# The last two loads of w2 in a decode kernel, each issued as two loads over parts of the partitions

## The chip, the core and the metric

The kernel runs on one core of a Trainium2 chip. The time is device time in microseconds (us) of that core for one execution. The core has a matrix engine (TensorE: PE for its products, PEld for the loading of its stationary operand), VectorE (DVE), ScalarE (ACT), GpSimd (POOL) and SyncE (SP), which here issues the transfers. Transfers between HBM and the on-chip memory are carried by 16 DMA engines. The on-chip memory has 128 partitions.

## The reference

One decode step for two batch rows: grouped attention over the last W = 4096 positions of a cache, a Mish feed-forward layer, and a gate that mixes the two.

```python
W = min(4096, max(256, Sk // 4))
q = (x @ wq) as (B, 32 heads, 1, 128)
k = jnp.repeat(k_cache[:, :, Sk - W:, :], 4, axis=1)
v = jnp.repeat(v_cache[:, :, Sk - W:, :], 4, axis=1)
p = softmax(einsum("bhqd,bhkd->bhqk", q, k) * Dh ** -0.5)
a = einsum("bhqk,bhkd->bhqd", p, v) as (B, 1, 4096) @ wo
h = x @ w1 + b1
b = (h * tanh(softplus(h))) @ w2
g = sigmoid((x * gate_w).sum(-1))
out = g * a + (1 - g) * b
```

All is float32. w2 is 1792 by 512: 14 blocks (f = 0 to 13) of 128 rows, and a block is 256 KB.

## The kernel before

Some 91 MB have to be read, and the kernel is a stream of loads that SP issues in the order of the program: wq in two halves, a small tile, w1, then for each of eight key/value heads a K and a V tile of 4 MB, then w2 and wo. A big load writes a tile of 128 partitions from one of five stream buffers; SP issues it when the buffer's last readers are done.

The end of the stream is cut ever finer, so that little work is left behind the last byte: `w2_0` (blocks 0 to 9 of w2, 2.5 MB), wo in four pieces (`wo0` 4 MB, `wo4` 2 MB, `wo6` and `wo7` 1 MB each), and then the tail of w2 in three pieces that have their own tiles and wait for no buffer: `w2_10` (blocks 10 and 11, 512 KB), `w2_12` and `w2_13` (one block, 256 KB each). CUTS holds these cuts of w2. In such a load a partition gets one contiguous run, 2 KB in the last two.

TensorE follows in the same order. `project` sums the products with w2_0 and wo into `acc`, four column groups side by side. When wo7's products are done, ACT and then DVE copy half of `acc` each into `asum`. `finish` sums into a second accumulator, `fin`: first the eight products with w2_10, then four that fold asum in, then four with w2_12, then four with w2_13. Four small copies (DVE and ACT in turn) bring fin into `res`, and SP issues the store of res to `out`.

Each load signals its arrival on one of eight semaphores (here DMAHW0 to DMAHW7), which the loads take in turn; SP issues a load on a semaphore only when the load that had it before has arrived. The row names below leave the numbers out: `w` is a piece of w1 or w2, `wo` a piece of wo.

Of the kernel before, what the change touches and what calls it, by code (L numbers as in the profile page):

```python
# [13 lines left out]
P = 128  # L14
# [20 lines left out]
SMALL = DC * B + DC + FC  # L35
SCALE = DH ** -0.5
CUTS = (0, 10, 12, 13, 14)


@with_exitstack  # L40
def decode_kernel(ctx: ExitStack, tc: tile.TileContext, small, wq, kt, v, wo, w1, w2, out):
    nc = tc.nc
# [8 lines left out]
    def load(src, cols, name):  # L51
        t = stream.tile([P, CHUNK], F32, tag="s", name=name)
        nc.sync.dma_start(t[:, :cols], src)  # L53
        return t
# [90 lines left out]
    def values(kv, pT, t):  # L145
        o = ps_1.tile([P, BN, DH], F32, tag="o", name=f"o{kv}")
        for c in range(NT):
            for j in range(NJ):
                nc.tensor.matmul(o[Q * j : Q * j + Q], pT[:, c, Q * j : Q * j + Q],  # L149
                                 t[:, (c * NJ + j) * 512 : (c * NJ + j + 1) * 512],  # L150
                                 start=(c == 0), stop=(c == NT - 1))
        d = od[:, kv, :]
        nc.vector.tensor_scalar_mul(d, o[:, 0, :], pick[:, 0:1])  # L153
        for m in range(1, BN):
            nc.vector.scalar_tensor_tensor(d, o[:, m, :], pick[:, m : m + 1], d,  # L155
                                           op0=ALU.mult, op1=ALU.add)
# [98 lines left out]
    def load_w2(i):  # L255
        f0, f1 = CUTS[i], CUTS[i + 1]
        src = w2[f0 * P * D : f1 * P * D].rearrange("(p x) -> p x", p=P)
        if i == 0:
            return load(src, (f1 - f0) * D, f"w2_{f0}")
        t = const.tile([P, (f1 - f0) * D], F32, name=f"w2_{f0}")  # L260
        nc.sync.dma_start(t, src)
        return t

    def load_wo(k0, k1):
        return load(wo[k0 * REP * D * P : k1 * REP * D * P].rearrange("(p x) -> p x", p=P),
                    (k1 - k0) * REP * D, f"wo{k0}")

    w2_0 = load_w2(0)
    wos = [(k0, k1, load_wo(k0, k1)) for k0, k1 in ((0, 4), (4, 6), (6, 7), (7, 8))]
    tail = [load_w2(i) for i in range(1, len(CUTS) - 1)]  # L270

    acc = ps_1.tile([P, D], F32, tag="acc", name="acc")
# [3 lines left out]
    def project(j, lhsT, rhs, n):  # L276
        nc.tensor.matmul(acc[Q * j : Q * j + Q, :], lhsT, rhs,  # L277
                         start=(n_col[j] == 0), stop=(n_col[j] == n - 1))
        n_col[j] += 1

    n_of = [HKV + len(range(j, CUTS[1], NJ)) for j in range(NJ)]
    n_fin = FC - CUTS[1] + 1
    done = [0]
# [11 lines left out]
    values(HKV - 1, pT, last_v)  # L295
    for f in range(CUTS[1]):
        project(f % NJ, actT[:, f, :], w2_0[:, f * D : (f + 1) * D], n_of[f % NJ])
# [10 lines left out]
    def output(i):  # L308
        for f in range(CUTS[i], CUTS[i + 1]):
            x = (f - CUTS[i]) * D  # L310
            finish(actT[:, f, :], tail[i - 1][:, x : x + D])
# [53 lines left out]
```

## Time and profile before

| | us |
|---|---|
| median of 3 runs | 221.48 (221.29 to 222.4) |
| the profiled execution, its own time | 221.49 |
| its span, first to last instruction | 219.70 |
| TensorE busy in the span | 123.8 (56%) |
| VectorE busy | 36.5 (17%) |
| ScalarE busy | 9.1 (4%) |
| DMA queue of the loads, share of 16 engines | 96.8% |

The own time is 1.79 us more than the span, for what lies before the first and behind the last instruction. The busy times overlap; the last line says how much of the span the 16 DMA engines had packets of the loads under way. Two things are to be looked up in such a profile for a change at the end of a stream: when the last bytes arrive, and what the engines do between that and the last instruction.

### The profile page before, as it was taken

Reading aid. Unit: us, or ns where it says so; the run is one execution under the profiler, and the core shown is the slowest. Engines: PE = TensorE matmul, PEld = TensorE weight load, DVE = VectorE, ACT = ScalarE, POOL = GpSimd, SP = SyncE. Lnnn points to the kernel's source line nnn. Section 1 sums busy time; section 2 is a strip of 40 time slices with the busy share of each in tenths; the row PEclk is TensorE's granted clock in tenths of the full one; section 3 lists DMA queues with packets and bytes.
Section 4 is the critical chain, followed back from the end, with each engine's and each line's share of the span. In section 5 each row is a group of like instructions: output and inputs, shape, how many; then the busy total and the mean of one; then the engine's idle time right before and its main releaser. Section 6 shows DMA issues by size and latency. Waiting matters only on the chain.

```text
span 219.7 us, 1885 instructions
## 1 busy us (share of the span) xinstructions
PE 123.8 (56%) x798; PEld 37.0 (17%) x798; DVE 36.5 (17%) x132; ACT 9.1 (4%) x23; POOL 3.0 (1%) x9
## 2 busy tenths in 40 slices
PE   0058638265473628576392752668474655695763
PEld 0012212012120201211020120112011111521112
DVE  1011212411202200120202112011211205302001
ACT  2000000010001000100100010010001001000001
POOL 5000000000000000000000000000000000000000
PEclk9999988887969976676969799585888879679999
DMA  7999999999999999999999999999999999999990
GB/s 280 406 462 397 454 431 427 441 419 465 400 465 394 462 400 459 412 447 430 430 444 418 453 412 453 406 465 403 453 406 453 424 436 407 440 462 403 409 381 22
DMA packets 4043, 91.35 MB, mean 416 GB/s; under 512 B 578, under 2 KB 578, under 8 KB 964
## 3 DMA queue, kind: packets, MB, share of 16 engines
q1 hardware_dynamic: 4036, 91.25, 96.8%
q8 instruction: 6, 0.10, 0.2%
q14 instruction: 1, 0.01, 0.0%
HBM read 91.24 MB, written 0.00 MB: 415 GB/s over the span
## 4 chain that ended last, share of the span: by engine, by line
DMA 80%; PE 15%; DVE 2%; ACT 1%; SPq 1%; issue 1%; DVEq 0%
DMA k<-in_kt 40%; DMA w<-in_w 21%; DMA v<-in_v 19%; PE sc L130 5%; PE o L149 4%; PE hp L208 2%; PE ol L195 1%; PE fin L287 1%; SPq L53 1%; ACT p L137 0%; DVE mx L133 0%; DVE pT L142 0%; PE pp L141 0%; DVE res L321 0%; DVE r L188 0%
## 5 line engine op out<-in xcount | busy, mean ns | idle before, releaser
L130 PE MATMUL sc<-k,qz 128*32 128x512 f32 x256 | 43.1, 836 | 36.1 <-DMA k<-in_kt 36.1
L149 PE MATMUL o<-v,pT 128*32 128x512 f32 x256 | 40.5, 790 | 12.1 <-DMA v<-in_v 11.3
L130 PEld LDWEIGHTS sc<-k,qz 128*32 128x32 f32 x256 | 9.9, 147 | 68.8 <-DMA k<-in_kt 42.8
L149 PEld LDWEIGHTS o<-v,pT 128*32 128x32 f32 x256 | 10.5, 140 | 36.6 <-issue 34.0
L133 DVE TENSOR_REDUCE mx<-sc 128x1 f32<-128x512 f32 x8 | 5.5, 692 | 65.2 <-PE sc L130 65.2
L112 PE MATMUL qp<-wqa,x 128*32 128x512 f32 x32 | 6.6, 763 | 13.5 <-DVE x L79 13.5
L141 PE MATMUL pp<-ident,p 128*128 128x128 f32 x32 | 5.5, 297 | 14.4 <-ACT p L137 14.4
L137 ACT ACTIVATE p<-sc,bias 128x512 f32<-128x512 f32 x8 | 5.5, 687 | 140.1 <-DVE bias L135 121.1
L153 DVE TENSOR_SCALAR od<-o,pick 128x128 f32<-128x128 f32 x8 | 2.8, 351 | 47.7 <-PE o L149 47.7
L277 PE MATMUL acc<-wo,oT 128*32 128x512 f32 x64 | 7.7, 598 | 4.2 <-DMA wo<-in_wo 4.2
L155 DVE SCALAR_TENSOR_TENSOR od<-o,pick,od 128x128 f32<-128x128 f32 x24 | 8.4, 351 | 0.8
L142 DVE COPY pT<-pp 128x512 f32<-128x512 f32 x8 | 5.5, 692 | 11.8 <-PE pp L141 11.7
L208 PE MATMUL hp<-w,x 128*32 128x512 f32 (+1 forms) x32 | 5.3, 765 | 3.4 <-DMA w<-in_w 3.4
L141 PEld LDWEIGHTS pp<-ident,p 128*128 128x128 f32 x32 | 3.4, 141 | 21.0 <-ACT p L137 21.0
L195 PE MATMUL ol<-kf,od 128*128 128x8 f32 x16 | 3.5, 350 | 2.3 <-DVE od L155 1.6
L112 PE MATMUL qp<-wqb,x 128*32 128x512 f32 x32 | 3.6, 594 | 0.9 <-DMA wqb<-in_wq 0.9
L112 PEld LDWEIGHTS qp<-wqa,x 128*32 128x32 f32 x32 | 1.2, 136 | 16.2 <-DVE x L79 13.5
L195 PEld LDWEIGHTS ol<-kf,od 128*128 128x128 f32 x16 | 3.4, 312 | 3.4 <-DVE od L155 2.6
L277 PEld LDWEIGHTS acc<-wo,oT 128*32 128x32 f32 x64 | 1.7, 109 | 10.2 <-DMA wo<-in_wo 5.5
L306 DVE COPY asum<-acc 128x256 f32<-128x256 f32 x1 | 0.4, 425 | 14.8 <-ACT asum L305 14.8
L208 PEld LDWEIGHTS hp<-w,x 128*32 128x32 f32 x32 | 1.7, 143 | 6.4 <-issue 6.4
L277 PE MATMUL acc<-w,actT 128*32 128x512 f32 x20 | 2.8, 597 | 0.0
(76 smaller groups left out, 33.4 us busy)
## 6 DMA issues: line engine op xcount, KB each, us to landing
k<-in_kt SPq DMA_DIRECT2D x8, 4096.0 KB, 43.0
v<-in_v SPq DMA_DIRECT2D x8, 4096.0 KB, 43.1
wqa<-in_wq SPq DMA_DIRECT2D x1, 4096.0 KB, 12.3
wqb<-in_wq SPq DMA_DIRECT2D x1, 4096.0 KB, 21.2
wo<-in_wo SPq DMA_DIRECT2D x1, 4096.0 KB, 39.7
w<-in_w SPq DMA_DIRECT2D x1, 3584.0 KB, 29.2
w<-in_w SPq DMA_DIRECT2D x1, 2560.0 KB
wo<-in_wo SPq DMA_DIRECT2D x1, 2048.0 KB, 34.6
```

The lines of the kernel that those rows point to most:

```text
L112: nc.tensor.matmul(qp[Q * k : Q * k + Q, :], x32[:, c, :], w[:, c, k, :], start=(c == 0), stop=(c == DC - 1))
L130: nc.tensor.matmul(sc[Q * j : Q * j + Q, :], qz[:, kv, m * Q : m * Q + Q], t[:, (m * NJ + j) * 512 : (m * NJ + j + 1) * 512], start=(m == ...
L133: nc.vector.tensor_reduce(mx[:, kv : kv + 1], sc, axis=AX.X, op=ALU.max)
L137: nc.scalar.activation(p, sc, AF.Exp, bias=bias, scale=SCALE, accum_out=ls[:, kv : kv + 1])
L141: nc.tensor.transpose(pp[:, c, :], p[:, c * P : (c + 1) * P], ident)
L142: nc.vector.tensor_copy(pT, pp)
L149: nc.tensor.matmul(o[Q * j : Q * j + Q], pT[:, c, Q * j : Q * j + Q], t[:, (c * NJ + j) * 512 : (c * NJ + j + 1) * 512], start=(c == 0), s ...
L153: nc.vector.tensor_scalar_mul(d, o[:, 0, :], pick[:, 0:1])
L155: nc.vector.scalar_tensor_tensor(d, o[:, m, :], pick[:, m : m + 1], d, op0=ALU.mult, op1=ALU.add)
L195: nc.tensor.matmul(ol[:, kv].rearrange("p b h -> p (b h)"), od[:, kv, :], kf[:, kv, :], start=True, stop=True)
L208: nc.tensor.matmul(hp[Q * j : Q * j + Q, :n], x32[:, c, :], w[:, c, j * FG * P : j * FG * P + n], start=(c == 0), stop=(c == DC - 1))
L277: nc.tensor.matmul(acc[Q * j : Q * j + Q, :], lhsT, rhs, start=(n_col[j] == 0), stop=(n_col[j] == n - 1))
```

## The change

A table PARTS says for each piece of w2 over which partitions its load is cut. w2_10 stays one load over all 128. w2_12 becomes a load over partitions 0 to 103 and one over 104 to 127; w2_13 becomes one over 0 to 119 and one over 120 to 127. The tiles, their contents and what reads them stay as they are.

```diff
 CUTS = (0, 10, 12, 13, 14)
+PARTS = (None, (P,), (104, P), (120, P))
...
         t = const.tile([P, (f1 - f0) * D], F32, name=f"w2_{f0}")
-        nc.sync.dma_start(t, src)
+        p0 = 0
+        for p1 in PARTS[i]:
+            nc.sync.dma_start(t[p0:p1], src[p0:p1])
+            p0 = p1
         return t
```

On SP, the end of the queue of issues before the change; the brackets name the semaphores that an issue waits for, and the numbers behind the names are buffers:

```order
L53 DMA wo0_615<-in_wo 128x8192 [waits DMAHW0_49,PE_49]
L53 DMA wo4_617<-in_wo 128x4096 [waits DMAHW1_49,PE_49]
L53 DMA wo6_619<-in_wo 128x2048 [waits DMAHW2_49,PE_49]
L53 DMA wo7_621<-in_wo 128x2048 [waits DMAHW3_49,PE_49]
L261 DMA w2_10_623<-in_w2 128x1024
L261 DMA w2_12_625<-in_w2 128x512
L261 DMA w2_13_627<-in_w2 128x512
L322 DMA out_0<-res_795 2x512 [waits DMAHW4_49,Activation_49]
```

The same place with the change:

```order
L264 DMA w2_10_623<-in_w2 128x1024
L264 DMA w2_12_625<-in_w2 104x512
L264 DMA w2_12_625<-in_w2 24x512
L264 DMA w2_13_628<-in_w2 120x512 [waits DMAHW4_49]
L264 DMA w2_13_628<-in_w2 8x512 [waits DMAHW5_49]
L326 DMA out_0<-res_797 2x512 [waits DMAHW6_49,Activation_49]
```

There are two issues more. Since each load takes the next of the eight semaphores, the third and fourth part now come round to two that are in use: DMAHW4 is that of w2_0, DMAHW5 that of wo0.

On TensorE, the last rows of the program (`fin`) before the change:

```order
L287 MATMUL fin_630<-asum_772,fold_86 32x128 [waits DVE_49]
L287 MATMUL fin_630<-asum_772,fold_86 32x128
L287 MATMUL fin_630<-w2_12_625,actT_101 32x128 [waits DMAHW2_49]
L287 MATMUL fin_630<-w2_12_625,actT_101 32x128 x3
L287 MATMUL fin_630<-w2_13_627,actT_101 32x128 [waits DMAHW3_49]
L287 MATMUL fin_630<-w2_13_627,actT_101 32x128 x3
```

And with it:

```order
L291 MATMUL fin_632<-asum_774,fold_86 32x128 [waits DVE_49]
L291 MATMUL fin_632<-asum_774,fold_86 32x128
L291 MATMUL fin_632<-w2_12_625,actT_101 32x128 [waits DMAHW3_49,DMAHW2_49]
L291 MATMUL fin_632<-w2_12_625,actT_101 32x128 x3
L291 MATMUL fin_632<-w2_13_628,actT_101 32x128 [waits DMAHW5_49,DMAHW4_49]
L291 MATMUL fin_632<-w2_13_628,actT_101 32x128 x3
```

The order of the products is the same. The first product with w2_12, and the first with w2_13, each wait for two semaphores in place of one.

## Rows read from the trace of the kernel before

**Rows 1.** The page's head and its part on the DMA queues.

```profile
span 219.7 us, 1885 instructions
DMA packets 4043, 91.35 MB, mean 416 GB/s; under 512 B 578, under 2 KB 578, under 8 KB 964
q1 hardware_dynamic: 4036, 91.25, 96.8%
q8 instruction: 6, 0.10, 0.2%
```

**Rows 2.** Chain that ended last, its end: start us, us, what.

```profile
198.15 16.25 DMA w<-in_w
214.40 0.04 issue
214.44 1.77 PE fin L287 x40
216.22 0.02 issue
216.24 0.29 DVE res L321
```

**Rows 3.** Stretches of 0.2 us: us, DVE busy, PEclk, DMA share, GB/s.

```profile
213.00:213.20 0.20, 0.00 (x0) 1.00 1.00 399
...
213.40:213.60 0.20, 0.00 (x0) 1.00 0.71 277
213.60:213.80 0.20, 0.00 (x0) 1.00 0.48 184
...
214.00:214.20 0.20, 0.00 (x0) 1.00 0.45 174
...
214.60:214.80 0.20, 0.00 (x0) 1.00 0.38 143
214.80:215.00 0.20, 0.20 (x1) 1.00 0.26 102
...
215.20:215.40 0.20, 0.03 (x1) 1.00 0.06 20
215.40:215.60 0.20, 0.00 (x0) 1.00 0.00 0
```

**Rows 4.** The line that issues the tail of w2: forms, waits, landing.

```profile
L261 SPq DMA_DIRECT2D w<-in_w x3: 424/425/432, 198.2 to 199.1; - x3
DMA to landing us min/median/max: 16.2/16.5/16.6
```

**Rows 5.** Timeline of the end (start us, us, engine line ..., idle before).

```profile
213.27 1.07 PE L277 MATMUL acc<-wo,oT 128*32 128x512 f32 x8 [1.46 <-DMA wo<-in_wo]
...
214.40 0.37 ACT L305 COPY asum<-acc 128x256 f32<-128x256 f32 x1 [27.02 <-PE acc L277]
...
214.80 0.42 DVE L306 COPY asum<-acc 128x256 f32<-128x256 f32 x1 [14.79 <-ACT asum L305]
```

**Rows 6.** Timeline of PEld, 215.3 to 215.7: fold and w2_12.

```profile
215.28 0.11 PEld L287 LDWEIGHTS fin<-asum,fold 128*32 128x32 f32 x2 [0.26 <-DVE asum L306]
...
215.32 0.32 PEld L287 LDWEIGHTS fin<-w,actT 128*32 128x32 f32 x6
```

**Rows 7.** Timeline of PEld, from 215.7: w2_13.

```profile
215.74 0.16 PEld L287 LDWEIGHTS fin<-w,actT 128*32 128x32 f32 x8
```

**Rows 8.** TensorE's separate waits on line 277, ns min/median/max.

```profile
L277 PEldq EVENT_SEMAPHORE  x2: 51/51/51, 199.3 to 213.2; - x2
```

**Rows 9.** Timeline from 203: the first products with wo0.

```profile
203.39 1.07 PE L277 MATMUL acc<-wo,oT 128*32 128x512 f32 x8 [0.96 <-DMA wo<-in_wo]
```

**Rows 10.** The store's issue in the timeline.

```profile
217.44 0.32 SPq L322 DMA_DIRECT2D out<-res  x1
```

**Rows 11.** SP's own waits: engine line, waited for, us, times, longest.

```profile
SPq L361 <- DMA out<-res: 0.8, 1, 0.8
```

## The prediction, made before the changed kernel was run

> **What bounds the kernel now.** The page's head says most of it: 91.35 MB at a mean of 416 GB/s is the whole span, and the load queue keeps the 16 DMA engines under way for 96.8% of it [rows 1]. A change that moves no byte fewer can only act at the end, on what lies between the last bytes and the last instruction. So I read the chain that ended last, then the last microseconds in stretches of 0.2 us, then the timeline of the engines there.
>
> The chain ends in a transfer of a piece of w2 that arrives at 214.40, then 1.77 us of TensorE on `fin`, then the copies [rows 2]. That piece is w2_10, the first of three issued from 198.15 on; they land 16.2 to 16.6 us after their issues, which begin 198.2 to 199.1 [rows 2, 4]. So w2_13 arrives at 199.1 + 16.6 = 215.7. The chain merges all of `fin` into one piece and so hides whether TensorE stood still again for w2_13. The reader is to check that in the weight loads.
>
> There two things meet. On the side of the sums: wo7's products end at 213.27 + 1.07 = 214.34, the ACT half of asum at 214.77, the DVE half at 215.22 [rows 5], the last fold begins at 215.28, and w2_12's weight loads follow behind it at once and end at 215.32 + 0.32 = 215.64 [rows 6]. On the side of the transfers: w2_13's first weight load starts at 215.74 [rows 7], 0.04 us after the landing worked out above. TensorE therefore waits 0.10 us for w2_13. **However early w2_13 came, the end could move by 0.10 us only**, since the asum path, which the change doesn't touch, would then set it.
>
> The stretches show that the sixteen DMA engines don't stop together. The DMA share is 1.00 at 213.1, falls to 0.48 by 213.7, stays at 0.45 at 214.1 and 0.38 at 214.7, is 0.26 at 214.9 and 0.06 at 215.3 [rows 3]. Times 16: all, then about 8, 7, 6, 4, and 1 engine. About nine have done their share by 213.6, six work some 1.4 us longer, and one ends last, near 215.3; its landing is seen at 215.7. So the arrival of a load is that of its latest engine. The trace doesn't number the engines.
>
> **The change, part by part.**
>
> *Where the rows go.* A row here is the 2 KB of one partition. At 416 / 16 = 26 GB/s an engine needs 2048 B / 26 GB/s = 0.079 us for one [rows 1]. Before, the last two loads are 128 rows each, 8 to an engine if all sixteen share alike, as the full share up to 213.2 suggests. The new parts divide into equal whole shares as 104 = 13 x 8, 24 = 12 x 2, 120 = 15 x 8 and 8 = 8 x 1. Read so, each part starting at the same engine, which is my assumption, one engine loses 16 rows (1.26 us), two lose 8 (0.63 us), one keeps its 16, four get 2 more (0.16 us) and eight get 3 more (0.24 us).
>
> The Trainium skill (DMA: Bandwidth & Descriptors, section "Why a DMA increments its semaphore by 16 and not by 1") states for loads issued by SP that the number of engines is the largest divisor, at most 16, of the outermost size, and that the lowest-numbered are used. By it the counts are the same, with engine 15 as the one that loses most; no row here shows it, so the sum below doesn't use it.
>
> *What it does to the arrival of w2_13.* The nine early engines can take 0.24 us unseen: they have 1.4 us to spare [rows 3]. Bounds for the late ones: if the last engine is among those that get more, the arrival goes from 215.70 to 215.94 at most, +0.24 us, all of it seen, since TensorE already waits there. If it is one of the three relieved, the other late ones (through at about 215.0) set the arrival, with up to 0.24 more at about the time of before; at the very best all that are left come earlier, and the end gains the 0.10 us of the asum bound. So -0.10 to +0.24. Nothing in the rows says which engines are late; twelve of sixteen get more and three get less, so by count 12/16 x 0.2 - 3/16 x 0.1 = +0.13; I take +0.1.
>
> *Two more semaphore waits on TensorE.* The first products with w2_12 and with w2_13 wait for two semaphores each. TensorE has such a pair before wo7, and the separate wait that it brings is an instruction of 51 ns [rows 8]. Two of them cost between nothing (issued ahead, while products are running) and 0.10 us. I take 0.05: the one before w2_13 has a standstill to lie in, the one before w2_12 stands right behind the asum wait.
>
> *Two more issues on SP.* An issue of the tail takes 424 to 432 ns [rows 4]; two are 0.86 us, and SP is through at 200.5 instead of 199.5 if nothing holds it. But the fourth part waits for the semaphore of wo0, whose first product starts at 203.39 [rows 9], so the part is issued at about 203.4 and out of SP by 203.9. Queued behind it on SP is the store of the result alone, at 217.44 [rows 10]. The part's rows stand behind all others and are due after 213. The cover is over 9 us; without it (had it to wait for wo7, at 213.27) an issue of 0.43 us and a way of at most 1.2 us (below) would land it at 214.9, still no later than the rest. The wait for w2_0 is long over. I cost both at nothing.
>
> *The sum.* 221.49 of the profiled execution + 0.1 + 0.05 = 221.64, from bounds of -0.10 to +0.34, that is 221.39 to 221.83. The median of the runs, 221.48, is 0.01 below the profiled one, so the forecast is **221.6 us**: no change that can be measured. Half a per cent, 1.1 us, is about what a measurement of this kernel can tell from none, and the three runs of before lie as far apart.
>
> **Rivals.**
>
> *The late engines are the relieved ones.* Then the tail of rows 3 gets shorter and the arrival earlier, up to 0.3 us. For it: one engine ends alone, and one engine is relieved most. Against a visible gain: the asum bound. 221.49 - 0.10 + 0.05 = about 221.4.
>
> *The shares don't change.* If the parts are spread in some finer way, all engines stop as before: 221.5.
>
> *The parts go to eight engines.* (The slower side.) All four sizes divide by 8. Dealt to eight engines, they would bring 13 + 3 + 15 + 1 = 32 rows each in place of 16, 16 x 0.079 = 1.26 us more. On the early engines that is 213.6 + 1.26 = 214.9 and hidden; on the last one the arrival is 215.7 + 1.26 = 216.96 and the time 221.49 + 1.26 + 0.05 = 222.8, +0.6%. It decides from 1.1 us on, 14 extra rows on the last engine. Against it: that it needs both, this dealing and the last engine among the eight.
>
> *Each small load costs a fixed time.* From the issue of the store, 4 KB into an empty queue, at 217.44, to the end of SP's wait for it are 0.32 + 0.8 = 1.1 us, 1.2 with the gap between [rows 10, 11]. Two such at the tail would be 2.4 us: 223.9. The Trainium skill speaks for this side (same page, "Rules for kernel authors": don't split a transfer over disjoint partitions, since both halves use the same engines, and under 64 KB one mostly pays overhead); the second and fourth part are 48 and 16 KB. The rows speak against: the three loads of the tail, issued 0.43 us apart, land within 215.7 - 214.4 = 1.3 us for 512 KB, 400 GB/s [rows 4], so queued loads don't pay it one after the other.
>
> *Faster by over 0.5%.* Needs 1.1 us, against an asum bound of 0.10. It would take another course of the six instruction fetches that share the DMA engines [rows 1], or a misread bound.
>
> **How the numbers follow.** Forecast (the last engine gets a little more, 221.6): 0.55. The late ones relieved (221.4): 0.31. Shares unchanged (221.5): 0.05. Eight engines, and it shows (222.8): 0.03. Fixed cost (223.9): 0.03. Faster by something else: 0.03. The first three are within 0.5%: 0.91; slower 0.06; faster 0.03. The sum's bounds, 221.4 to 221.8, are narrower than the runs of one and the same kernel, which go from 0.2 below their median to 0.9 above; widened by 0.4 below and 0.5 above the range is 221.0 to 222.3.
>
> **What would show it.** In the stretches of the last 2 us: the early engines stop up to 0.24 us later, the share behind 214.0 falls by one to three engines if late ones are relieved. w2_13's first weight load at 215.8 to 216.0 says loaded, at 215.65 to 215.75 relieved; at 217 it is the eight engines. The fold at 215.28 and the end of wo7's products at 214.34 should stay: if they move, a term is missing. SP should show the fourth part's issue at about 203.4. A time under 220.4 or over 222.6 would make the forecast wrong.

## The result, and the profile after

| | before | with the change |
|---|---|---|
| median, us | 221.43 (221.16 to 222.4, 10 runs) | 222.41 (222.19 to 223.21, 10 runs) |
| profiled execution, its own time | 221.49 | 222.27 |
| its span | 219.7 | 220.5 |

The ratio is 1.0043, 95% interval 1.0028 to 1.0057: 0.98 us slower by the medians, small but clear of zero, and just beyond the upper end of the range (222.3). The forecast was no change, with a sum of +0.15 us.

The page's head and its line on the load queue, which answer to [rows 1]:

```profile
span 220.5 us, 1889 instructions
DMA packets 4059, 91.35 MB, mean 414 GB/s; under 512 B 594, under 2 KB 594, under 8 KB 980
q1 hardware_dynamic: 4052, 91.25, 96.8%
```

There are 16 packets more, all of them under 512 B (578 before), and those under 8 KB grow by the same 16, so the data rows are as many as before. If each engine that takes part in a load ends it with one small packet, the two loads of before bring 2 x 16 = 32 and the four parts 13 + 12 + 15 + 8 = 48: the difference is 16. The trace also keeps the signals with which the engines report the end of a load: 16 each for w2_12 and w2_13 before, and 13, 12, 15 and 8 for the four parts. The numbers of engines that the prediction assumed are borne out, and with them the rule that the Trainium skill states for these numbers (DMA: Bandwidth & Descriptors, "Why a DMA increments its semaphore by 16 and not by 1"). Which of the engines they are, the trace doesn't show.

The end of the chain that ended last (start us, us, what), beside [rows 2]:

```profile
198.07 17.21 DMA w<-in_w
215.28 0.04 issue
215.32 0.86 PE fin L291 x24
216.18 0.10 issue
216.28 0.87 PE fin L291 x16
217.15 0.02 issue
217.18 0.29 DVE res L325
```

The piece whose arrival stands in this chain is **w2_10, which the change doesn't touch**. It arrives at 215.28 in place of 214.40, 0.88 us later, and the first copy into res starts 0.94 us later.

The weight loads from there on (timeline of PEld; start us, us, engine line ..., idle before), beside [rows 6, 7]:

```profile
215.32 0.38 PEld L291 LDWEIGHTS fin<-w,actT 128*32 128x32 f32 x16 [1.82 <-DMA w<-in_w]
215.67 0.24 PEld L291 LDWEIGHTS fin<-asum,fold 128*32 128x32 f32 x8
216.25 0.19 PEld L291 LDWEIGHTS fin<-w,actT 128*32 128x32 f32 x8 [0.34 <-DMA w<-in_w]
216.68 0.16 PEld L291 LDWEIGHTS fin<-w,actT 128*32 128x32 f32 x8 [0.24 <-DMA w<-in_w]
```

Before, TensorE had only the last wait here after the fold, of 0.10 us. Now it waits for w2_10 until 215.32, does the fold behind it at 215.67 (215.28 before), waits for w2_12 0.34 us and for w2_13 until 216.68 (215.74 before). So all three pieces come late by about the same, and the last one sets the end. asum is not what holds it: wo7's products and the two copies stand where they stood, 0.07 us later, beside [rows 5]:

```profile
213.34 1.07 PE L281 MATMUL acc<-wo,oT 128*32 128x512 f32 x8 [1.67 <-DMA wo<-in_wo]
214.46 0.37 ACT L309 COPY asum<-acc 128x256 f32<-128x256 f32 x1 [27.24 <-PE acc L281]
214.87 0.42 DVE L310 COPY asum<-acc 128x256 f32<-128x256 f32 x1 [14.95 <-ACT asum L309]
```

And the same stretches of 0.2 us as in [rows 3] (us, DVE busy, PEclk, DMA share, GB/s):

```profile
213.00:213.20 0.20, 0.00 (x0) 1.00 1.12 246
213.40:213.60 0.20, 0.00 (x0) 1.00 0.97 236
213.60:213.80 0.20, 0.00 (x0) 1.00 0.95 205
214.00:214.20 0.20, 0.00 (x0) 1.00 0.93 256
214.60:214.80 0.20, 0.00 (x0) 1.00 0.42 102
214.80:215.00 0.20, 0.13 (x1) 1.00 0.42 133
215.20:215.40 0.20, 0.09 (x1) 1.00 0.33 123
```

This is the reading that the rest hangs on. At 213.0 to 213.2 the share is full in both kernels (in so short a stretch it can come out above 1, as the 1.12 here), but the engines moved 399 GB/s before and 246 now; at 213.7 the share is 0.95 in place of 0.48, for 205 GB/s. **The engines are under way longer and carry less**: an engine at a full share moved 399 / 16 = 25 GB/s before and 246 / 16 = 15 GB/s now. A share of busy time alone looks healthy here; only the two columns together show it.

The records of the single packets, which the traces keep as well, say it row by row. Before, each of w2_10's 128 rows of 4 KB took 0.159 us, and each of the 256 rows of 2 KB behind them 0.084 us. With the change 38 of w2_10's rows took over a tenth longer than that, up to 0.376 us, and 147 of the 256 did, up to 0.213 us. Together the rows of the three pieces kept their engines for 52.3 us in place of 41.9: 0.65 us more for each of the sixteen.

### The profile page after: what moved, and what is told of

It is laid out like the page before. It is cut to its first block, busy times and chain, and to the rows that moved or that the text cites. A ratio compares the mean times of both kernels' runs of the same rounds, so it can differ in the third digit from the quotient of the medians.

```text
span 220.5 us, 1889 instructions
## 1 busy us (share of the span) xinstructions
PE 130.0 (59%) x798; PEld 38.2 (17%) x798; DVE 36.4 (17%) x132; ACT 9.1 (4%) x23; POOL 3.0 (1%) x9
## 4 chain that ended last, share of the span: by engine, by line
DMA 79%; PE 16%; DVE 2%; ACT 1%; SPq 1%; issue 1%; DVEq 0%
DMA k<-in_kt 39%; DMA w<-in_w 21%; DMA v<-in_v 19%; PE sc L131 5%; PE o L150 5%; PE hp L209 2%; PE ol L196 1%; PE fin L291 1%; SPq L54 1%; ACT p L138 0%; DVE mx L134 0%; DVE pT L143 0%; PE pp L142 0%; DVE res L325 0%; DVE r L189 0%
## 5 line engine op out<-in xcount | busy, mean ns | idle before, releaser
L131 PE MATMUL sc<-k,qz 128*32 128x512 f32 x256 | 43.8, 848 | 30.9 <-DMA k<-in_kt 30.9
L150 PE MATMUL o<-v,pT 128*32 128x512 f32 x256 | 46.0, 883 | 11.2 <-DMA v<-in_v 10.4
L150 PEld LDWEIGHTS o<-v,pT 128*32 128x32 f32 x256 | 11.7, 153 | 39.8 <-issue 35.6
```

The lines of the kernel that those rows point to most:

```text
L131: nc.tensor.matmul(sc[Q * j : Q * j + Q, :], qz[:, kv, m * Q : m * Q + Q], t[:, (m * NJ + j) * 512 : (m * NJ + j + 1) * 512], start=(m == ...
```

## The experiments

Three theories were set against each other. The *partition theory*: a load over a part of the partitions brings several engines onto the same way into the memory, and slows rows of neighbouring loads too. The *share theory*: some engines just have more rows. The *count theory*: each further load costs something fixed. The diffs are against the kernel with the change where they edit PARTS, and against the kernel before elsewhere.

**e1_columns.** As many loads and issues, but each half over all partitions. TensorE has as many waits, too, but in another form than the expectation says: four products wait for one half each, where the changed kernel has two products that wait for two parts each.

```diff
-        nc.sync.dma_start(t, src)
+        n = (f1 - f0) * D
+        for x0, x1 in ((0, n),) if i == 1 else ((0, n // 2), (n // 2, n)):
+            nc.sync.dma_start(t[:, x0:x1], src[:, x0:x1])
```

> w2_12 and w2_13 are each cut into two loads again, but over columns: both halves write all 128 partitions. Issues, semaphores and waits are those of the changed kernel, the rows are 1 KB. Three theories of the 0.96 us. Partition theory (mine): a load over a part of the partitions brings several DMA engines onto the same way into the memory, so that rows take longer, those of neighbouring loads too; then nothing is lost here: 221.3 to 221.7 us, w2_10 arrives near 214.4. Share theory (some engines get more rows): shares are equal here, 221.5. Count theory (each further load costs a fixed time at its arrival, its issue or its wait): as the changed kernel, 222.4.

Measured: 221.21 us (12 runs), ratio 0.9983 (0.9964 to 1.0002); before on the same chip 221.37. No loss. In its stretches the bytes keep up with the share:

```profile
213.00:213.20 0.20, 0.00 (x0) 1.00 1.12 420
213.20:213.40 0.20, 0.00 (x0) 1.00 1.09 405
213.60:213.80 0.20, 0.00 (x0) 0.50 0.67 241
```

The profiled execution was the slowest of the twelve, 222.38 us. The last of these rows shows why: while wo7's products ran, TensorE's granted clock fell to 0.50 (1.2 in place of 2.4 GHz), and its sums ended late (wo7's products took 1.65 us in place of 1.07). The transfers didn't: w2_10's weight loads begin at 214.42 (214.44 before), as the partition theory expected.

```profile
214.42 0.87 PEld L289 LDWEIGHTS fin<-w,actT 128*32 128x32 f32 x16 [1.02 <-DMA w<-in_w]
```

Two more issues, two more waits on TensorE and the changed semaphores cost nothing to be seen. The count theory falls. The median lies 0.1 us under what was expected, and the interval includes no change.

**e2_112_16.** A cut over partitions with equal shares.

```diff
-PARTS = (None, (P,), (104, P), (120, P))
+PARTS = (None, (P,), (112, P), (112, P))
```

> Both loads are cut at partition 112: 112 = 16 x 7 and 16 = 16 x 1, so that each engine has 8 rows of each block, as before. Share theory: no loss, 221.5 us. Count theory: 222.4. Partition theory: 222.0 or more, since partitions are dealt to the engines in sevens and ones in place of eights; the stretches from 213 to 214 show a DMA share near 1 at well under 300 GB/s, and w2_10 arrives later than 214.4.

Measured: 222.33 us (12 runs), ratio 1.0042 (1.0026 to 1.0057), the loss of the change itself. Its page has 4075 packets, 32 more than before, so all sixteen engines took part in all four parts (4 x 16 - 32). In the stretches:

```profile
213.00:213.20 0.20, 0.00 (x0) 1.00 0.86 205
213.40:213.60 0.20, 0.00 (x0) 1.00 0.93 246
213.60:213.80 0.20, 0.00 (x0) 1.00 1.02 236
```

w2_10's products begin at 215.34, as late as in the changed kernel. With equal shares the loss is whole, so it doesn't take unequal shares.

**e3_only_w2_12 and e4_only_w2_13.** One of the two cuts alone.

```diff
-PARTS = (None, (P,), (104, P), (120, P))
+PARTS = (None, (P,), (104, P), (P,))
```

> Only w2_12 is cut (104 and 24), w2_13 is one load. Partition theory: most of the loss stays, since the early engines write w2_12's part while the late ones still bring w2_10: w2_10 arrives near 215.2, the time is 222.0 to 222.4 us. Share theory: up to 0.24 us more on the last engine, 221.6. Count theory: half of the loss, 221.9.

```diff
-PARTS = (None, (P,), (104, P), (120, P))
+PARTS = (None, (P,), (P,), (120, P))
```

> Only w2_13 is cut (120 and 8), w2_12 is one load. Partition theory: w2_10 is nearly undisturbed (arrives before 214.8), the slow rows fall on w2_12's and w2_13's end, and the loss is smaller than in the changed kernel: 221.6 to 222.2 us. Share theory: 221.5. Count theory: 221.9, the same as with w2_12 alone.

Measured: w2_12 alone 222.22 us, 1.0029 (1.0013 to 1.0044); w2_13 alone 222.04 us, 1.0024 (1.0009 to 1.0039). Each cut costs a part, and the intervals don't tell the two apart; the medians are in the expected ranges. The profiled execution of e4 shows that even w2_13's parts, the last in the queue, reach back to w2_10 (timeline of PEld):

```profile
212.99 0.19 PEld L281 LDWEIGHTS acc<-wo,oT 128*32 128x32 f32 x8 [2.33 <-issue]
214.60 0.38 PEld L291 LDWEIGHTS fin<-w,actT 128*32 128x32 f32 x16 [1.43 <-DMA w<-in_w]
...
215.37 0.16 PEld L291 LDWEIGHTS fin<-w,actT 128*32 128x32 f32 x8 [0.17 <-DMA w<-in_w]
216.02 0.19 PEld L291 LDWEIGHTS fin<-w,actT 128*32 128x32 f32 x8 [0.50 <-DMA w<-in_w]
```

wo7's first weight loads before, and with the change:

```profile
213.24 0.19 PEld L277 LDWEIGHTS acc<-wo,oT 128*32 128x32 f32 x8 [2.34 <-issue]
...
213.31 0.19 PEld L281 LDWEIGHTS acc<-wo,oT 128*32 128x32 f32 x8 [2.55 <-issue]
```

From wo7's first weight load to w2_10's it is 214.60 - 212.99 = 1.61 us; before it is 214.44 - 213.24 = 1.20, with the change 215.32 - 213.31 = 2.01. "Nearly undisturbed" was too much said: some of the delay is there already. In e3's profiled execution TensorE's granted clock was 0.50 in the tail, as in e1's, so its weight loads aren't compared.

The landings, a load's last signals, can be compared in all six: e1's, at that clock, agree with those of before to 0.03 us (table in us; of a load cut in two, the later part).

| | wo7 | w2_10 | w2_12 | w2_13 | w2_10 behind wo7 | slow rows of w2_10 |
|---|---|---|---|---|---|---|
| before | 213.14 | 214.40 | 215.08 | 215.70 | 1.26 | 0 of 128 |
| e1, both over columns | 213.11 | 214.38 | 215.05 | 215.71 | 1.27 | 0 |
| e3, w2_12 over partitions | 213.38 | 215.08 | 216.02 | 216.46 | 1.70 | 35 |
| e4, w2_13 over partitions | 212.88 | 214.56 | 215.32 | 215.92 | 1.68 | 18 |
| e2, both at 112 | 213.18 | 215.30 | 215.91 | 216.54 | 2.12 | 33 |
| the change | 213.21 | 215.28 | 216.15 | 216.64 | 2.07 | 38 |

A slow row is one that took over a tenth longer than the 0.159 us that all of them took before. In these executions, one of each kernel, each cut over partitions holds w2_10 up by about 0.4 us, the two together by 0.8 to 0.9, and the cuts over columns by nothing.

The next six make the disputed cost large: they leave the tail alone and cut one 4 MB load of mid-stream, k3, where every engine is busy before, during and after.

**e5_mid_64_64.**

```diff
-        nc.sync.dma_start(t[:, :cols], src)
+        for p0, p1 in ((0, 64), (64, P)) if name == "k3" else ((0, P),):
+            nc.sync.dma_start(t[p0:p1, :cols], src[p0:p1])
```

> The tail is that of the kernel before; in mid-stream one 4 MB load (k3) is cut into partitions 0 to 63 and 64 to 127. Each engine has 4 rows of 32 KB of each part. Partition theory: in the changed kernel the tail moved about 205 GB/s at a full DMA share in place of 400; if both parts run at such a half rate, 4 MB take 20 us in place of 10: about 231 us. The Trainium skill (SBUF - State Buffer, Door 1: The DMA port swizzle) has it that 64 partitions in a row reach 8 of 16 ways into the memory. Share theory: no loss, 221.5. Count theory: under 0.5 us, 221.9 at most.

Measured: 233.75 us (4 runs), ratio 1.0538 (1.0488 to 1.0588): 12.4 us for cutting one load in two. Stretches of 5 us of the kernel before (columns as above):

```profile
85.00:90.00 5.00, 0.84 (x2) 0.84 1.06 459
90.00:95.00 5.00, 0.69 (x1) 0.50 0.99 426
95.00:100.00 5.00, 1.41 (x4) 0.84 0.99 426
100.00:105.00 5.00, 0.00 (x0) 0.67 0.97 419
105.00:110.00 5.00, 1.54 (x3) 1.00 1.00 433
110.00:115.00 5.00, 0.00 (x0) 0.66 0.99 423
```

The same stretches of this kernel:

```profile
85.00:90.00 5.00, 1.53 (x3) 1.00 1.18 393
90.00:95.00 5.00, 0.00 (x0) 0.56 1.06 203
95.00:100.00 5.00, 0.80 (x3) 0.75 0.98 210
100.00:105.00 5.00, 0.61 (x2) 0.93 1.03 210
105.00:110.00 5.00, 0.00 (x0) 0.50 0.98 210
110.00:115.00 5.00, 0.00 (x0) 0.50 0.86 321
```

A full share at half the bytes, 210 GB/s, for 20 us. Over the 30 us the difference is (2586 - 1547) GB/s x 5 us = 5.2 MB; at the 431 GB/s of before that is 12.0 us, close to the 12.4 that were timed. It is more than the 10 us expected, which reckoned half the rate for k3's 4 MB alone. The packets show the rest: k3 has 128 rows of 32 KB, but 159 such rows between 82 and 122 us took over a tenth longer than the usual 1.21 us (2.47 in the mean), so rows of neighbouring loads are among them.

**e6_mid_32_96.**

```diff
-        nc.sync.dma_start(t[:, :cols], src)
+        for p0, p1 in ((32, 96), (0, 32), (96, P)) if name == "k3" else ((0, P),):
+            nc.sync.dma_start(t[p0:p1, :cols], src[p0:p1])
```

> The same 4 MB load cut into partitions 32 to 95, 0 to 31 and 96 to 127: the first part has 64 partitions as in the run with 64 and 64, but other ones. If the ways into the memory are as the Trainium skill's table says (SBUF - State Buffer, Door 1: The DMA port swizzle), 32 to 95 reach all sixteen and run at full rate, and the two quarters reach eight each and run at half. Partition theory in that form: half of the bytes at half rate, +5 us, about 226.5 us. If it is the number of partitions in a load that makes it slow, whichever they are, it is as slow as 64 and 64 or slower. Share theory: 221.5. Count theory: under 1 us.

Measured: 227.81 us (4 runs), ratio 1.0270 (1.0233 to 1.0306): +6.5 us, half of e5's loss with one load more, and 1.3 us above the 226.5 expected. The stretches:

```profile
90.00:95.00 5.00, 0.49 (x1) 0.50 1.02 347
95.00:100.00 5.00, 1.40 (x4) 0.84 1.02 223
100.00:105.00 5.00, 0.00 (x0) 0.50 0.95 216
105.00:110.00 5.00, 0.00 (x0) 0.51 0.95 387
```

The low stretch is half as long. So the cost isn't that of 64 partitions as such; it depends on which. What e5's expectation says of 64 partitions in a row goes for 0 to 63 and 64 to 127, and not for 32 to 95.

**e9_to_32_96_from_0_64 and e10_to_0_64_from_32_96.** e5 and e6 differ both in the partitions written and in the rows read. These two swap the sources. Both give up the order of one key tile's rows and serve for the time alone.

```diff
-        nc.sync.dma_start(t[:, :cols], src)
+        for p0, s0, n in ((32, 0, 64), (0, 64, 32), (96, 96, 32)) if name == "k3" else ((0, 0, P),):
+            nc.sync.dma_start(t[p0:p0 + n, :cols], src[s0:s0 + n])
```

> k3 is again cut into three loads. They write the partitions of the run with 32 to 95 first, but the first of them reads rows 0 to 63 of the source, which the run with 64 and 64 read first (the rows of this one key tile thereby stand in another order, which changes its scores). If the rate hangs on the partitions that are written, the time is that of the run with 32 to 95: 227 to 228.5 us. If it hangs on what is read from HBM, the first part is slow too and the time is that of 64 and 64: 233 to 234.5.

```diff
+        for p0, s0, n in ((0, 32, 64), (64, 0, 32), (96, 96, 32)) if name == "k3" else ((0, 0, P),):
```

> The other way round: the parts write partitions 0 to 63, 64 to 95 and 96 to 127 and read rows 32 to 95, 0 to 31 and 96 to 127 of the source (order of this key tile's rows changed as before). If the written partitions decide, all parts run at half rate as with 64 and 64: 233 to 234.5 us. If the source decides, 227 to 228.5.

Measured: 228.01 us, 1.0300 (1.0269 to 1.0332), and 234.31 us, 1.0585 (1.0496 to 1.0673), from two runs each. e9 goes with e6 and e10 with e5: the partitions that are written decide, not the rows that are read.

**e7_mid_104_24.** The cut of w2_12, on k3.

```diff
-        nc.sync.dma_start(t[:, :cols], src)
+        for p0, p1 in ((0, 104), (104, P)) if name == "k3" else ((0, P),):
+            nc.sync.dma_start(t[p0:p1, :cols], src[p0:p1])
```

> The same 4 MB load cut as w2_12 is in the change, 104 and 24. Share theory: twelve engines have 10 rows of 32 KB in place of 8; at 26 GB/s a row is 1.26 us, so +2.5 us: 224 us. Partition theory: rows are slower besides, +5 us at the least and up to +14: 226 to 235. Count theory: under 0.5 us.

Measured: 240.07 us (4 runs), ratio 1.0833 (1.0784 to 1.0881): +18.7 us, above all that was expected. Stretches in mid-stream and near the end:

```profile
90.00:95.00 5.00, 0.50 (x1) 0.50 1.02 210
110.00:115.00 5.00, 0.00 (x0) 0.50 0.91 144
...
225.00:228.00 3.00, 0.00 (x0) 1.00 0.80 332
228.00:231.00 3.00, 0.00 (x0) 1.00 0.80 325
```

The rate is halved as in e5, and at the end the share is 0.80 for six microseconds: 0.8 x 16 = 13, so about three engines had run out of work while the others went on. That is the share theory's effect, and it is there as well; the larger part is the rate. In the seven stretches of 5 us from 85 to 120 us this kernel moved 6.4 MB less than the one before, which at 431 GB/s is 15 of the 18.7 us.

**e8_mid_columns.** The control.

```diff
-        nc.sync.dma_start(t[:, :cols], src)
+        for x0, x1 in ((0, cols // 2), (cols // 2, cols)) if name == "k3" else ((0, cols),):
+            nc.sync.dma_start(t[:, x0:x1], src[:, x0:x1])
```

> The control of the three: the same 4 MB load cut into two halves of its columns, each over all 128 partitions. Partition and share theory: no loss, 221.3 to 221.7 us. Count theory: up to 0.5 us more.

Measured: 221.36 us (10 runs), ratio 0.9985 (0.9968 to 1.0002). A cut over columns costs nothing here either. The slow rows of 32 KB, counted as in e5, sort the runs as the times do: 1 before and 1 here, 94 and 96 in e6 and e9, 159 and 161 in e5 and e10, 178 in e7.

## Why the prediction was wrong

*What bounds the kernel.* Right as far as it went: the stream ends the kernel, asum's path stood still (0.07 us), and TensorE waits for the tail.

*Where the rows go.* The numbers of engines were right, by the 16 further small packets and the signals. **The step that failed is the price of a row, "At 416 / 16 = 26 GB/s an engine needs 2048 B / 26 GB/s = 0.079 us for one".** For loads over all 128 partitions it holds (0.084 us by the packets), but it was carried over to parts as if an engine's speed were its own. In the tail of the changed kernel the sixteen engines at a full share moved 246 and 205 GB/s; 2048 B at 246 / 16 = 15 GB/s are 0.13 us, at 205 / 16 = 13 GB/s 0.16 us; by the packets the 256 rows took 0.11 us in the mean and up to 0.213. e2 has the loss with the old shares, e1 has none with the new count, and e9 and e10 tie the rate to the partitions written, for k3's cuts in mid-stream; the tail's own cuts weren't tried with other sources.

A rule that points this way stands in the Trainium skill, on a page that the prediction didn't weigh: SBUF - State Buffer, "Door 1: The DMA port swizzle", by which 16 ports lead into the memory, and partitions 0 to 63 in a row reach only eight of them. The runs with cut halves agree: 210 GB/s in e5 against 431, and half of that loss in e6, whose first part reaches all sixteen by that table. The loss of the change itself doesn't follow from the table alone, by which partitions 0 to 103 already reach all sixteen. Which engine writes which partitions of 104 and 24 or of 112 and 16 no trace shows, since none numbers the engines; which of them met there stays open.

*The arrival of w2_13, "-0.10 to +0.24".* It landed at 216.64 in place of 215.70, and its weight loads start 0.94 us later. The bound also took it that only w2_12 and w2_13 could come late. **The parts slowed w2_10 too**, which was to arrive at 214.40 as before: that it does so only where later loads are cut is shown (e2, e3, e4, and not e1), and so is that rows of w2_10 itself took longer. That early engines at the parts slow late ones still at w2_10 is read from the times: the share is about 1 from 213.0 to 213.8, and the first slow row of w2_10 starts at 212.63, 0.7 us behind the first row of a part (211.93). The prediction's sentence that the early engines "can take 0.24 us unseen" counted their own spare time and not what they do to the others.

*Two more waits on TensorE, two more issues on SP.* Both priced rightly at next to nothing. e1 has the issues, at no loss. The separate waits that the pairs bring are two of 51 ns, as forecast, and stand where TensorE waits for landings anyway; w2_13's weight loads start 0.04 us after its landing (216.64), as they did before (215.70). SP's fourth part was to be issued at about 203.4, held by wo0; the timeline of SP has it at 203.30 and in no one's way (the line behind it is that of the two waits, ns min/median/max):

```profile
203.30 0.27 SPq L264 DMA_DIRECT2D w<-in_w  x1
...
L291 PEldq EVENT_SEMAPHORE  x2: 51/51/51, 216.2 to 216.3; - x2
```

*The rivals.* None named the cause. The one on eight engines had a right consequence, more time on the engines, by a dealing that didn't happen (13, 12, 15 and 8 signals); that its 222.8 lies nearer than the forecast is luck. The one of a fixed cost for each small load was given 2.4 us and falls with e1 and e8 as far as loads of 128 KB and more go. Against it for the 48 and 16 KB here speak the landings: the 48 KB part came 0.20 us behind the 208 KB one (215.95), and the 16 KB part at 216.24, before the 240 KB one at 216.64. Neither is near the 1.2 us for a load. The Trainium skill's rule cited there, not to split over disjoint partitions, came out right here, but not as an overhead of each load: the cuts over columns make as many loads and lose nothing.

*What would show it.* The fold was named as a place that "should stay: if they move, a term is missing". It moved, from 215.28 to 215.67, while asum stood, and that pointed at w2_10. w2_13's first weight load, at 216.68, lies in none of the places that were named for it (215.65 to 215.75, 215.8 to 216.0, 217). The time stays under the 222.6 that was to make the forecast wrong, but it lies above its range, and the way there is another.

## What to carry to other kernels

If a load is to be cut, cut it over its columns and not over its partitions: here the same number of loads cost nothing one way and up to half the rate of the stream the other. A price per row taken from whole loads holds for whole loads only. And in the tail of a stream the neighbours count: a load that is not touched can be the one that comes late, so compare GB/s with the DMA share, not the share alone.

## What the runs showed of the hardware that was not expected

Cutting a single 4 MB load over partitions cost 12.4 us (64 and 64), 6.5 us (32 to 95, then the quarters) and 18.7 us (104 and 24), at 203 to 223 GB/s with a DMA share of about 1 in the low stretches (144 GB/s at 0.91 in one of the last). With equal shares of rows, seven and one to an engine, the tail lost as much as with unequal ones (222.33 against 222.41 us). A load that wasn't cut had rows of up to 0.376 us in place of 0.159, for two cut loads behind it in the queue.
